# The stores of split rows move from SyncE's queue to GpSimd's, in an attention and two-network kernel

## The chip, the cores and the metric

The kernel runs on one core of a Trainium2 chip. The metric is the device time of the core in microseconds (us). Three runs of the kernel before took 730.86 to 731.88 us, with a median of 731.15. Short names of the engines: PE is TensorE, DVE is VectorE, ACT is ScalarE, POOL is GpSimd and SP is SyncE, which only issues DMAs here.

## The reference

Sparse attention feeds two dense networks, all in float32:

```
attn: 4 batches x 8 heads, 576 positions, head size 64, masked (local for 4 heads, strided for 4)
x   = attention output as 2304 tokens x 512
h   = max(x @ w1, x @ w2, x @ w3)        # first network, 512 -> 768
x2  = h @ w_out                          # 768 -> 512
h   = x2 @ w_in                          # second network, 512 -> 2048
g   = max(h, 0) + alpha * min(h, 0)
out = g @ w_out                          # 2048 -> 512
```

## The kernel before, in words

Each float32 factor of a matmul is held as a pair of a high part (a rounded copy) and a low part (what the rounding left), each [128, n]. A product is three matmuls per block: high x high, high x low, low x high (`PAIRS`). A split of rows is therefore two steps: a cast to the high part, and a subtraction for the low part.

The first network works batch by batch. Attention and the first three batches are ordered by a planner (`Weave`), which is over at about 300 us. The last batch is written out by hand in `last_net`: twelve gate units, 42 products (`product`, L913), and eight output products (L762) whose results are the tokens x2. They go to DRAM.

A product of `last_net` is 6 matmuls, an output product 18. Their results come in PSUM banks, eight of which are used in turn. The 42 products are six groups of seven. The first result of a group is copied by ACT (L931); the others are added and compared by DVE (L893). The last group ends in rows of h, split by ACT (L926, high) and DVE (L900, low). Every output product reads all rows of h, those of the last group last.

The second network works on three blocks of 768 tokens, numbered 0, 1 and 2, by a scheme of seven products for a 2 x 2 block matrix (`PRODUCTS`). Its x side needs seven row combinations for each of two halves, so fourteen split tiles of [128, 2, 384] per block. For block 0 they are made just before use. For blocks 1 and 2 they are made early, stored to DRAM (`xd`) and fetched again (`fetch_x2`, L1026) shortly before the block begins. A split tile is 384 KB.

Block 1's fourteen are made in the loop around `last_net`, in two halves. `early_load` (L982, SP) loads four pieces of x2 rows into two tiles `xs`, `early_sums` (L991) makes four sums on POOL, in part in the tiles `xs` themselves, and `early_split` casts a high part on ACT (L233) and subtracts the low part on POOL (L236), for seven parts numbered 0 to 6. The split tiles `xst` come from two pools of two buffers, used in turn: the cast of part k waits until the store of part k - 4 has landed. One unit of `last_net` after each split, `early_store` (L1020) issues its store. The second half's `early_load` goes into the same two tiles `xs`, so it waits for the low parts of the first half. The same pool `xsp`, and `xst`, later hold the x2 rows for block 0 (`load_x2`, L982).

Block 2's fourteen are made inside the second network, a step at a time: high part on ACT (L1443), some steps later the low part on DVE (L1435), and at its end `early_store`.

Each engine runs its own instructions in program order, and so does SP's queue of DMA issues: an issue that waits holds those behind it. SP issues every DMA of this kernel: weights (L852 for the last batch, L1034 and L1046 for the second network), rows, stores of x2 (L773) and of the result (L1193).

Of the kernel before, what the change touches and what calls it, by code (L numbers as in the profile page):

```python
# [10 lines left out]
F32 = mybir.dt.float32  # L11
# [161 lines left out]
def attention_maxout_prelu_kernel(  # L173
# [13 lines left out]
    nc = tc.nc  # L187
# [54 lines left out]
    def pool(stack, name, bufs, side="left"):  # L242
# [6 lines left out]
    xd = [None] + [[[dram.tile([P, 2, HB], F32, name=f"xd{blk}_{k}_{i}") for i in range(2)]  # L249
                    for k in range(7)] for blk in range(1, NBLK)]  # L250
# [766 lines left out]

    def early_store():
        for blk, k, i, t in early_parts:
            nc.sync.dma_start(xd[blk][k][i], t.bitcast(F32))  # L1020
        early_parts.clear()

    def fetch_x2(blk, k):
# [93 lines left out]
    for n, _ in enumerate(last_net(B - 1)):  # L1117
        if n in fetched:
            load_ow()
        if n - 1 in ready:  # L1120
            early_store()
        for half in range(2):
            if n == X_SPLIT + 21 * half - 8:
                early_load(1, half, xsp, "xs")
            if n == X_SPLIT + 22 * half - 2:
                early_sums(1, half)
        if n in ready:
            early_split(*ready[n], (xst, xsu)[n // 2 % 2])
        if n == gates - 5:
            rows = [load_x2(0, 0, xsp, "xs"), load_x2(0, 1, xst, "xst")]  # L1130
        if n == gates - 1:
            sx.close()
            x0x.close()
            xmp = pool(ctx, "xmp", 1, "right")
        if n == gates:
            sum_x2(0, 0, rows[0], nc.vector)
        if n == gates + 1:
            sum_x2(0, 1, rows[1], nc.vector)
        for i, ks in {0: [(0, range(7))], 2: [(1, range(4))], 3: [(1, range(4, 7))]}.get(n - gates, []):
            for k in ks:  # L1140
                x2h[0, k, i] = split_x2(0, k, i, xmp, f"x{k}{i}")
# [291 lines left out]
    def low_part(half, k):  # L1433
        t, x = high_parts.pop((half, k))
        nc.vector.tensor_tensor(out=t[:, 1], in0=x, in1=t[:, 0].bitcast(F32), op=ALU.subtract)  # L1435
        early_parts.append((2, k, half, t))
        if (half, k) != (0, 6):
            early_store()
# [12 lines left out]
    for half in range(2):  # L1451
        for n, i in steps[half][:4]:
            at(n, i, lambda: sums_left.pop(0)())
        for k, (n, i) in enumerate(steps[half][4:]):
            at(n - (i == 1), 4 if i == 1 else 2, lambda half=half, k=k: high_part(half, k))
            at(n, i, lambda half=half, k=k: low_part(half, k))
    at(NQ - 1, 0, early_store)

    outs = iter(())
    for n in range(NQ * NBLK):  # L1460
        blk, q = divmod(n, NQ)
# [72 lines left out]
```

## Time and profile before

| | |
|---|---|
| median of three runs | 731.15 us |
| profiled execution | 731.31 us, of which 729.5 us span |
| PE busy | 716.4 us (98%) |
| DVE busy | 615.0 us (84%) |
| ACT busy | 446.0 us (61%) |
| POOL busy | 30.3 us (4%), 53 instructions |
| DMA | 214.46 MB, mean 294 GB/s; nearly all on one queue, SP's |
| stores of split rows | 28 issues from SP of 384 KB |

The span goes from the first instruction to the last; the rest of an execution's time lies around it. Busy shares are means over the whole span. What an engine waits for is told in the waits and, in the timeline, in brackets behind an instruction: how long its engine stood idle before it, and what released it.

### The profile page before, as it was taken

The numbers are of one execution on the slowest core, as the hardware profiler recorded it, in microseconds if no ns is written. First come the engines' busy times: TensorE is split into PE (matmuls) and PEld (weight loads), VectorE is DVE, ScalarE is ACT, GpSimd is POOL, SyncE is SP. The second block draws the span as 40 slices with busy tenths as digits, with TensorE's granted clock in tenths as the row PEclk, the third lists the DMA queues.
The fourth block names the chain that finished last, engine by engine and source line by source line (L and its number), as shares of the span: only waits on it lengthen the run. The fifth ranks groups of instructions, "written<-read, shape, count | busy, mean of one in ns | idle before, by whom it ended". The sixth has DMA issues, their size and how long they took to land.

```text
span 729.5 us, 18174 instructions
## 1 busy us (share of the span) xinstructions
PE 716.4 (98%) x6682; PEld 698.0 (96%) x6682; DVE 615.0 (84%) x1680; ACT 446.0 (61%) x1180; POOL 30.3 (4%) x53
## 2 busy tenths in 40 slices
PE   8999999999999999899999999999999999999998
PEld 5899999999999999899989999999999999999997
DVE  6998987988989997588678988979988888888896
ACT  7988975876784784243356675626566644656561
POOL 2000000000000000065000000000000000000000
PEclk9999999999999999999999999999999999999999
DMA  8777599879999688698999799999789999867362
GB/s 296 271 274 232 176 310 344 312 277 308 327 358 343 229 278 290 224 319 321 367 331 339 250 332 328 404 392 357 252 301 318 370 400 354 302 228 264 108 201 68
DMA packets 90089, 214.46 MB, mean 294 GB/s; under 512 B 11152, under 2 KB 41360, under 8 KB 90000
## 3 DMA queue, kind: packets, MB, share of 16 engines
q1 hardware_dynamic: 90000, 213.30, 82.8%
q8 instruction: 53, 0.87, 0.5%
q14 instruction: 36, 0.29, 0.1%
HBM read 157.16 MB, written 56.10 MB: 292 GB/s over the span
## 4 chain that ended last, share of the span: by engine, by line
PE 92%; DVE 3%; ACT 3%; DMA 2%; issue 1%; SPq 0%; DVEq 0%; ACTq 0%
PE ph L1369 24%; PE bank L740 24%; PE po L1170 15%; PE bank L762 10%; PE bank L913 4%; PE po L1176 4%; PE ph L1170 4%; PE po L1180 2%; PE bank L426 1%; DMA wp<-w 1%; PE bank L352 1%; PE bank L465 1%; ACT es L487 1%; PE bank L535 1%; DMA raw<-in_w 1%
## 5 line engine op out<-in xcount | busy, mean ns | idle before, releaser
L740 PE MATMUL bank<-x,w 128*128 128x288 f32 x1440 | 199.4, 298 | 3.4 <-DVE t L751 3.2
L1369 PE MATMUL ph<-x,w 128*128 128x384 f32 x990 | 199.6, 336 | 0.8 <-ACT xo L969 0.8
L740 PEld LDWEIGHTS bank<-x,w 128*128 128x128 f32 x1440 | 193.5, 190 | 5.2 <-DVE t L751 3.5
L1369 PEld LDWEIGHTS ph<-x,w 128*128 128x128 f32 x990 | 166.6, 188 | 1.8 <-ACT xo L969 1.0
L1170 PE MATMUL po<-w,g 128*128 128x256 f32 x936 | 135.9, 282 | 0.0
L1170 PEld LDWEIGHTS po<-w,g 128*128 128x128 f32 x936 | 130.1, 190 | 0.3
L1375 DVE TENSOR_TENSOR c<-ph,c 128x384 f32<-128x384 f32 x165 | 89.3, 554 | 30.6 <-PE ph L1369 27.0
L1163 ACT CAST g<-c 128x384 fp32r<-128x384 f32 x93 | 47.0, 505 | 90.8 <-DVE c L1353 51.6
L762 PE MATMUL bank<-h,w 128*128 128x288 f32 x576 | 80.0, 297 | 0.0
L762 PEld LDWEIGHTS bank<-h,w 128*128 128x128 f32 x576 | 77.0, 189 | 0.4
L286 DVE TENSOR_TENSOR w<-word,w 128x512 fp32r<-128x512 f32 x100 | 63.6, 643 | 13.2 <-ACT w L283 12.5
L283 ACT CAST w<-word 128x512 fp32r<-128x512 f32 x100 | 57.6, 587 | 24.7 <-DMA wp<-w 8.5
L1313 ACT ACTIVATE c<-c 128x384 f32<-128x384 f32 x96 | 50.6, 527 | 32.9 <-DVE c L1375 31.8
L1314 ACT ACTIVATE c<-c,nalpha 128x384 f32<-128x384 f32 x96 | 59.3, 618 | 3.1
L1318 DVE SCALAR_TENSOR_TENSOR c<-c 128x384 f32<-128x384 f32 x96 | 53.0, 552 | 5.9 <-ACT c L1314 5.9
L1164 DVE TENSOR_TENSOR g<-c,g 128x384 fp32r<-128x384 f32 x96 | 52.9, 551 | 0.9 <-ACT g L1163 0.5
L1164 DVE TENSOR_TENSOR g<-k,g 128x384 fp32r<-128x384 f32 x72 | 37.0, 552 | 7.4 <-ACT g L1163 7.4
L1176 PE MATMUL po<-w,g 128*128 128x512 f32 x120 | 42.8, 396 | 0.0
L590 ACT ACTIVATE word<-raw 128x512 f32<-128x512 f32 x56 | 36.8, 675 | 5.7 <-DMA raw<-in_w 4.6
L830 DVE TENSOR_TENSOR t<-bank,t 128x288 f32<-128x288 f32 x72 | 32.6, 453 | 7.8 <-PE bank L740 3.8
L1353 DVE TENSOR_TENSOR k<-c 128x384 f32<-128x384 f32 x72 | 37.9, 550 | 0.0
L1163 ACT CAST g<-k 128x384 fp32r<-128x384 f32 x72 | 33.1, 514 | 7.1 <-PE po L1176 3.3
(123 smaller groups left out, 898.4 us busy)
## 6 DMA issues: line engine op xcount, KB each, us to landing
w<-wh SPq DMA_DIRECT2D x72, 512.0 KB, 5.4
raw<-in_w SPq DMA_DIRECT2D x50, 512.0 KB, 5.0
w<-wo SPq DMA_DIRECT2D x48, 512.0 KB, 5.9
w<-wp SPq DMA_DIRECT2D x36, 512.0 KB, 5.8
wh<-w SPq DMA_DIRECT2D x24, 512.0 KB, 4.8
xd<-xst SPq DMA_DIRECT2D x28, 384.0 KB, 3.0
x<-xd SPq DMA_DIRECT2D x28, 384.0 KB, 8.3
ws<-w SPq DMA_DIRECT2D x12, 512.0 KB, 4.6
```

Of the source, the lines that this page charges most:

```text
L283: (nc.scalar.copy if e == "ACT" else nc.vector.tensor_copy)(out_, in_)
L286: nc.vector.tensor_tensor(out=out_, in0=x, in1=y, op=ALU.subtract)
L740: nc.tensor.matmul(acc, words["gate", f, g][:, wi, cc * P:(cc + 1) * P], xt[b, cc, hf][:, xi, :], start=n == 0, stop=n == 3 * NCC - 1)
L762: nc.tensor.matmul(acc, words["mix", f][:, wi, dc * P:(dc + 1) * P], st["h", hf, f][:, xi, :], start=n == 0, stop=n == 3 * NF1 - 1)
L1163: cast(g[:, 0], x)
L1164: return g, lambda: nc.vector.tensor_tensor(out=g[:, 1], in0=x, in1=g[:, 0].bitcast(F32), op=ALU.subtract)
L1170: nc.tensor.matmul(bank[:, NH * half:NH * (half + 1)], g[:, gi, t * P:(t + 1) * P], w[:, wi, off:off + NH], start=first and i == 0, stop=l ...
L1176: nc.tensor.matmul(bank.rearrange("p (s n) -> p s n", n=NH), g[:, 0, t * P:(t + 1) * P], w[:, :, off:off + NH], start=first, stop=last)
L1314: nc.scalar.activation(a, a, AF.Copy, scale=nalpha[:, f:f + 1])
L1318: nc.vector.scalar_tensor_tensor(out=a, in0=h, scalar=0.0, in1=a, op0=ALU.max, op1=ALU.add)
L1369: nc.tensor.matmul(bank, words["h", n, i][:, wi, off + c * P:off + (c + 1) * P], x2h[blk, k, c][:, xi, :], start=m == 0, stop=m == 5)
L1375: nc.vector.tensor_tensor(out=out_, in0=bank, in1=other, op=ALU.add)
```

## The change

The function `early_store` issues its DMAs from POOL's queue and no longer from SP's. Its calls stay where they were, so on POOL the store of a part of block 1 stands between that part's low part and the next one's. Both uses are changed: block 1's stores and block 2's.

```diff
     def early_store():
         for blk, k, i, t in early_parts:
-            nc.sync.dma_start(xd[blk][k][i], t.bitcast(F32))
+            nc.gpsimd.dma_start(xd[blk][k][i], t.bitcast(F32))
         early_parts.clear()
```

## Rows read from the trace of the kernel before

**Rows 1.** The page, part 1: busy us (share of the span) and instructions of each engine.

```profile
PE 716.4 (98%) x6682; PEld 698.0 (96%) x6682; DVE 615.0 (84%) x1680; ACT 446.0 (61%) x1180; POOL 30.3 (4%) x53
```

**Rows 2.** Chain of waits in order of time: start us, length us, what.

```profile
319.40 30.42 PE bank L913 x227
349.82 17.13 PE bank L762 x129
```

**Rows 3.** Timeline of PE, 300 to 376 us: start, length, instruction, [idle before <-releaser].

```profile
318.87 30.95 PE L913 MATMUL bank<-x,w 128*128 128x288 f32 x228 [0.40 <-ACT x L233]
349.65 19.26 PE L762 MATMUL bank<-h,w 128*128 128x288 f32 x144
369.67 2.37 PE L1369 MATMUL ph<-x,w 128*128 128x384 f32 x12 [0.76 <-ACT xo L969]
372.59 2.36 PE L1369 MATMUL po<-x,w 128*128 128x384 f32 x12 [0.55 <-ACT xo L969]
```

**Rows 4.** Stretches: length, PE, PEld, DVE, ACT, POOL busy (x), clock, DMA, GB/s.

```profile
308.60:320.00 11.40, 10.78 (x65) 10.34 (x66) 9.06 (x20) 5.88 (x17) 5.54 (x6) 0.85 0.92 331
400.00:420.00 20.00, 20.00 (x136) 20.00 (x135) 18.55 (x39) 12.45 (x25) 0.00 (x0) 1.00 0.74 256
```

**Rows 5.** Line 1020: ns min/median/max, first and last start; waiter; landing.

```profile
L1020 SPq DMA_DIRECT2D xd<-xst x28: 319/320/548, 318.4 to 567.2; - x28
...
  ACT xst L233: 7.0, 6
...
DMA to landing us min/median/max: 2.3/3.0/7.6
```

**Rows 6.** Waits of SP's queue: us in total, times, longest.

```profile
SPq L1020 <- DVE xst L1435: 24.7, 13, 2.5
...
SPq L1020 <- POOL xst L236: 19.3, 11, 7.5
```

**Rows 7.** Timeline of POOL, 306 to 372 us; L991 sums, L236 low parts.

```profile
319.94 1.03 POOL L236 TENSOR_TENSOR xst<-t,xst 128x384 fp32r<-128x384 f32 x1 [1.54 <-ACT xst L233]
...
324.97 1.23 POOL L236 TENSOR_TENSOR xst<-xs,xst 128x384 fp32r<-128x384 f32 x1
335.71 1.02 POOL L991 TENSOR_TENSOR t<-xs 128x384 f32<-128x384 f32 x1 [9.50 <-DMA xs<-x]
...
340.12 1.02 POOL L236 TENSOR_TENSOR xst<-xs,xst 128x384 fp32r<-128x384 f32 x1
...
342.07 1.24 POOL L236 TENSOR_TENSOR xst<-xs,xst 128x384 fp32r<-128x384 f32 x1
...
346.98 1.01 POOL L236 TENSOR_TENSOR xst<-xs,xst 128x384 fp32r<-128x384 f32 x1 [0.31 <-ACT xst L233]
```

**Rows 8.** Timeline of ACT, 306 to 372 us.

```profile
328.33 0.40 ACT L931 COPY t<-bank 128x288 f32<-128x288 f32 x1 [3.43 <-PE bank L913]
...
346.39 0.51 ACT L233 CAST xst<-xs 128x384 fp32r<-128x384 f32 x1 [1.30 <-DMA xd<-xst]
...
356.67 0.51 ACT L233 CAST x<-xs 128x384 fp32r<-128x384 f32 x1 [3.02 <-DMA xs<-x]
```

**Rows 9.** Timeline of SP's issues, 306 to 372 us.

```profile
326.60 2.78 SPq L982 DMA_DIRECT2D xs<-x  x4
...
353.18 3.32 SPq L982 DMA_DIRECT2D xst<-x  x4
```

**Rows 10.** Line 982, the four loads issued at 306.1 to 308.7 us: landing.

```profile
DMA to landing us min/median/max: 2.3/2.4/2.5
```

**Rows 11.** Line 982, the last two loads, issued from 328.2 us: durations; landing.

```profile
L982 SPq DMA_DIRECT2D xs<-x x2: 452/572/693, 328.2 to 328.9; - x2
...
DMA to landing us min/median/max: 6.7/6.8/6.8
```

**Rows 12.** Timeline of DVE, 346 to 352.5 us.

```profile
347.23 1.02 DVE L893 TENSOR_TENSOR t<-bank,t 128x288 f32<-128x288 f32 x2 [0.24 <-ACT t L931]
...
351.21 0.45 DVE L900 TENSOR_TENSOR h<-t,h 128x288 fp32r<-128x288 f32 x1
```

## The prediction

> **What bounds the kernel now.** I read the page's busy shares first: TensorE (PE) is busy 716.4 of 729.5 us, POOL 30.3 us in 53 instructions [rows 1]. The chain of waits comes next: between 319.40 and 366.95 us it is two unbroken pieces of PE [rows 2]. Then PE's own timeline over 300 to 376 us: from 314 us on it stands 0.40, 0.76 and 0.55 us, each time for ScalarE (ACT) and never for a DMA [rows 3]. The stretches behind it show PE full, as in 400 to 420 us: 20.00 of 20.00 [rows 4]. So the stores can give back at most 0.40 + 0.76 + 0.55 = 1.71 us, and anything they delay far enough is paid in full.
>
> **The change part by part.** 28 issues of L1020 leave SP's queue and go to POOL's [rows 5]. On SP they took 0.32 us each, 9 us in all, and 24.7 + 19.3 us of waiting for the low parts [rows 5, 6], with other loads queued behind. PE waited for none of those loads [rows 3, 4], so this removal is worth nothing on the path; the loads' cover is their own buffers, issued several products ahead.
>
> *Fourteen stores of block 2* (414.5 to 567.2 us). POOL has nothing else there, 0.00 us in 400 to 420 us [rows 4]. High part on ACT, low part on DVE and the store are steps apart. ACT waited for a store six times, 7.0 us in all, and all six belong to block 1's cast (L233), the last at 346.39 [rows 5, 8]. Cost 0, hidden by an idle POOL and the distance between steps; without that cover each store would be late by D (below), and still not PE.
>
> *Fourteen stores of block 1* (from 318.4 us [rows 5] to 348). This is where POOL has work: it makes the four sums and the seven low parts of each half [rows 7], and each store now stands on POOL between one low part and the next. The unknown is D, how long a store holds POOL. From below, SP's 0.32 us; from above, POOL held until the data have landed, 3.0 us median [rows 5]. The nearest row is POOL's own instruction on this tile, 1.01 to 1.03 us and stretched to 1.24 [rows 7]. I take D = 1.1, a little over the unstretched ones for the hand-over, because the store becomes one more instruction of POOL, which serves this tile shape in that time.
>
> The Trainium skill gives a price that no row has: in "DMA: Bandwidth & Descriptors", section "Latency and other measured facts", a first byte comes after about 1 us from GpSimd's queue and about 0.6 us from SyncE's. With 1.0 for D the sum below would be 0.8 us shorter, an estimate from that page.
>
> First half. Low part 1 starts at 319.94 either way (store 0 fits into the 1.54 us of idle before it) and ends at 320.97. Then five stores and five low parts: 320.97 + 5 x (1.1 + 1.03) = 331.6, against 326.2 before (324.97 + 1.23) [rows 7]. ACT's casts for parts 4 to 6 wait for stores 0 to 2 and come some 2 us later; the next thing on ACT, the copy at 328.33, had waited 3.43 us for PE [rows 8], so this is absorbed. But the tiles that the low parts read are those that the next half's rows are loaded into (L982). Before, SP issued those at 326.60 to 329.4, they needed 6.7 us, and POOL's sums began at 335.71 [rows 7, 9, 11]. Now the second pair can't go before 331.6 and (0.45 us an issue, the shortest of these) 332.05. It finds a nearly empty queue, since SP has stood at that very wait, with only the first pair ahead of it; for the same load the rows have 2.4 us near 306 us and 6.7 us near 329 us [rows 10, 11]. I take 3.0, near the empty queue's row, as only the stores run beside it: the sums begin at 335.1, 0.6 us earlier than before, because the old queue was fuller.
>
> Second half. Sums 4.41 us (335.71 to 340.12 [rows 7]) end at 339.5. Three low parts with their stretches, 3.19 us (340.12 to 343.31), and two stores between them, 2.2 us: low part 2 ends at 344.9, its store leaves POOL at 346.0. Landing after that: SP's stores took 2.3 us at best and 3.0 median from issue [rows 5], 2.0 to 2.7 without the 0.32 us of issue; I take 2.4. So ACT's cast of part 6 starts at 348.4 in place of 346.39: 2.0 us late. As a formula, 339.57 + 8 x D against 346.39.
>
> What is queued behind it: ACT's copy (L931), for which DVE's add at 347.23 waited [rows 12]. DVE then runs without a gap worth the name to the low part of h that ends at 351.66 [rows 12]. The first output product starts at 349.65 and spends 0.134 us per matmul (19.26 over 144 [rows 3]); its 17th, at 351.79, reads that low part. Slack 0.1 us, so PE stands for 1.9 us. PSUM doesn't stop it before: with eight banks, the bank that the late copy frees is wanted by the second output product, at 352.1.
>
> After that: low part 6 ends at 354.0 (339.5 + 7.87 us for seven low parts, 340.12 to 347.99, + 6 x 1.1 us), store 6 lands at 357.5. Block 0's rows wait for those tiles: their last loads were issued by 356.5 [rows 9] and now go at about 358.3, 1.8 us later. That hides behind PE's own 1.9 us; without that stall it would be the next thing late, as PE waits for ACT at 369.67 already [rows 3].
>
> A rule could shorten this. Before, a store could take long behind loads in the same queue: 2.3 us at best, up to 7.6 [rows 5]. The Trainium skill ("DMA: Bandwidth & Descriptors", "Queues, rings and completion order") says that each DMA engine takes turns between queue rows, packet by packet, so a store in its own row would not stand behind SP's loads. By that rule landing would be at its 2.0 us, and the sum 0.4 us less. No run here shows it yet.
>
> Sum: +1.9 us on the path of the profiled execution, 729.5 of span plus 1.8 around it, 731.31 us. It lies 0.16 us over the median of 731.15, so 731.15 + 1.9 = 733.1 us.
>
> **The rivals.** (a) *POOL is held too briefly to matter.* With D near SP's 0.32 us the second half starts at 335.7 as before and the cast comes at 340.12 + 3.19 + 3 x 0.32 + 2.4 = 346.67, 0.3 us late: +0.2 us, 731.3. For it: SP's row. Against it: nothing on POOL that touches this tile takes under 1.0 us. (b) *POOL is held longer than one such instruction.* At D = 1.9 the formula gives 354.8, +8.3 us after the slack, 739.4; with rows landing in 6.7 in place of 3.0 us it is +5.6 at my own D. A stall of this size may also cost clock: between 308.6 and 320 us, where PE has just begun again after pauses, the granted clock is 0.85 over 11.4 us [rows 4], some 1.7 us. For it: eight D stand on the path, so each tenth of a microsecond is 0.8 us. (c) *Faster, by SP's freed queue.* Without 44 us of waiting on SP the rows for block 0 could land earlier, ACT's splits at 356.67 (3.02 us waiting for such rows [rows 8]) move up, and PE's pauses at 369.67 and 372.59 shrink. It decides if POOL's low parts end no later than before; the price is 1.3 us, 1.7 with the pause at 318.87, so 729.5 to 729.9. Against it: those loads are held by the low parts, which the stores push back. (d) *The change does nothing*, because SP's stores were hidden and POOL's are too, whatever D: that is (a)'s time, and the ACT waits of 7.0 us speak against it.
>
> **How the numbers follow.** Forecast 0.52 (+0.6 to +5 us, D of 0.95 to 1.45), (a) with (d) 0.26, (b) 0.14, (c) 0.08. A measurement of this kernel tells 0.2% (1.46 us) from no change. Of the forecast's chance 0.40 lies above that and 0.12 below. Slower: 0.40 + 0.14 = 0.54. Faster by over 1.46 us needs nearly all of the 1.71 us: 0.06 of (c). Same: 0.12 + 0.26 + 0.02 = 0.40. The range goes from 730.6 (within it all of (a)) to 737.5 (D near 1.7), leaving out (c)'s far end and most of (b). The forecast's own range is 731.7 to 736.
>
> **What would show it.** In the new profile: no L1020 on SP; starts of POOL's low parts 2.1 us apart in place of 1.0; the last one of the first half ending near 331.6 and the sums starting near 335.1; ACT's waits for the stores growing by some 2 us per half; a new PE wait of about 1.9 us in the first output product, on DVE's low part of h at L900; and PE otherwise as before up to the end. Low parts 1.3 us apart would be (a); over 2.8, (b). The prediction is wrong in its path if the casts come 2 us late and PE doesn't stop near 351.7, and wrong in its size if the spacing is right but the rows for the second half land at another time than 335.

## The result, and the profile after

The changed kernel took 740.4 us (median of 4 runs, 738.44 to 741.56), the kernel before, run beside it, 731.51 us (4 runs, 730.86 to 732.11). The ratio is 1.0119 with a 95% interval of 1.0095 to 1.0143: slower by 8.9 us, outside the predicted range. The profiled run took 738.44 us, 7.1 us more than before, with a span of 736.4 us.

The busy time of POOL grows as the change says, to 81 instructions [rows 1], and the 28 stores have a queue of their own, q0 (page, parts 1 and 3: queue, packets, MB, share of the 16 DMA engines):

```profile
PE 719.3 (98%) x6682; PEld 700.2 (95%) x6682; DVE 620.0 (84%) x1680; ACT 446.5 (61%) x1180; POOL 45.8 (6%) x81
...
q0 software_dynamic: 2240, 11.01, 3.7%
```

**Where PE lost it.** PE's timeline after, from 314 us, against [rows 3]:

```profile
314.82 3.34 PE L913 MATMUL bank<-x,w 128*128 128x288 f32 x24
318.74 30.96 PE L913 MATMUL bank<-x,w 128*128 128x288 f32 x228 [0.58 <-ACT x L233]
349.54 1.78 PE L762 MATMUL bank<-h,w 128*128 128x288 f32 x12
354.71 1.03 PE L762 MATMUL bank<-h,w 128*128 128x288 f32 x3 [3.40 <-ACT h L926]
356.53 20.40 PE L762 MATMUL bank<-h,w 128*128 128x288 f32 x129 [0.79 <-ACT h L926]
376.77 2.27 PE L1369 MATMUL ph<-x,w 128*128 128x384 f32 x12
```

Up to 349.54 us nothing is lost (349.65 before). Then PE stands in the first output product, where the prediction put it, for 3.40 + 0.79 us; and the 129 matmuls behind the stall take 20.40 us where before, at 19.26 us for 144, as many took 17.25. The runs below are compared by the stretch that holds all of this, from the first matmul of L913 to the first of L1369: 54.53 us before (315.14 to 369.67), 61.95 after. Of its growth of 7.42 us, 3.61 is idle time of PE (4.77 against 1.16) and 3.81 lies in the matmuls: 3.15 in the 129 behind the stall (20.40 against 17.25), and 0.63 in the three between the two waits, which take 1.03 us where 3 x 0.134 = 0.40 would do. The granted clock says why most of them are slower: it is between TensorE's two levels, 1.2 GHz (0.50) and 2.4 GHz (1.00), over the stretches from 350 us (columns as in [rows 4]), first before:

```profile
350.00:358.00 8.00, 8.00 (x62) 8.00 (x61) 3.65 (x10) 2.11 (x5) 0.00 (x0) 1.00 1.04 369
358.00:366.00 8.00, 8.00 (x63) 8.00 (x62) 6.99 (x14) 3.59 (x9) 0.00 (x0) 1.00 0.99 332
```

and after:

```profile
350.00:358.00 8.00, 3.69 (x17) 2.69 (x16) 5.86 (x14) 2.62 (x6) 3.69 (x5) 0.88 0.89 300
358.00:366.00 8.00, 8.00 (x46) 8.00 (x45) 7.25 (x16) 4.84 (x12) 0.00 (x0) 0.70 0.75 230
```

In the second line PE is busy all 8.00 us in both kernels, but does 46 matmuls in place of 63.

**What PE waited for.** The timeline of POOL after, against [rows 7]: L1020 is the store.

```profile
323.62 1.02 POOL L236 TENSOR_TENSOR xst<-t,xst 128x384 fp32r<-128x384 f32 x1
324.94 0.56 POOL L1020 DMA_DIRECT2D xd<-xst  x1 [0.30 <-POOL xst L236]
325.52 1.02 POOL L236 TENSOR_TENSOR xst<-xs,xst 128x384 fp32r<-128x384 f32 x1
...
330.06 1.02 POOL L236 TENSOR_TENSOR xst<-xs,xst 128x384 fp32r<-128x384 f32 x1
...
336.25 1.00 POOL L991 TENSOR_TENSOR t<-xs 128x384 f32<-128x384 f32 x1 [4.30 <-DMA xs<-x]
...
342.81 1.03 POOL L236 TENSOR_TENSOR xst<-t,xst 128x384 fp32r<-128x384 f32 x1
344.24 0.56 POOL L1020 DMA_DIRECT2D xd<-xst  x1 [0.41 <-POOL xst L236]
344.82 1.03 POOL L236 TENSOR_TENSOR xst<-xs,xst 128x384 fp32r<-128x384 f32 x1
```

A store costs POOL 0.56 us and, ahead of it, 0.30 to 0.41 us of waiting for the low part that POOL has just made: low parts are 1.9 us apart in the first half, 2.0 in the second. Then the timeline of ACT after, against [rows 8]: the casts of parts 4, 5 and 6, each waiting for a store to land, and the copy behind them.

```profile
347.97 0.51 ACT L233 CAST xst<-xs 128x384 fp32r<-128x384 f32 x1 [6.66 <-DMA xd<-xst]
350.14 0.51 ACT L233 CAST xst<-t 128x384 fp32r<-128x384 f32 x1 [1.66 <-DMA xd<-xst]
351.17 0.51 ACT L233 CAST xst<-xs 128x384 fp32r<-128x384 f32 x1 [0.51 <-DMA xd<-xst]
351.58 0.39 ACT L931 COPY t<-bank 128x288 f32<-128x288 f32 x1
```

And the landing of the three stores that they wait for (line 1020 after, issued from 342.2 to 346.3 us; the same three took 2.3, 2.3 and 3.0 us before):

```profile
DMA to landing us min/median/max: 4.8/5.7/5.8
```

Measured from the first matmul of L913, the cast of part 6 came at +31.25 us before and at +36.35 after, 5.10 later. That is 0.86 from the sums (+20.57, now +21.43), 2.21 from the spacing of the low parts (part 2: +26.93, now +30.00, 3.07 later), and 2.03 from the landing (from the start of low part 2 to the cast, 4.32 and now 6.35 us).

The last link is DVE. One of its steps in the timeline before, and the same stretch after, against [rows 12]:

```profile
348.29 0.46 DVE L893 TENSOR_TENSOR t<-t 128x288 f32<-128x288 f32 x1
```

```profile
352.01 1.02 DVE L893 TENSOR_TENSOR t<-bank,t 128x288 f32<-128x288 f32 x2 [1.80 <-ACT t L931]
353.06 1.13 DVE L893 TENSOR_TENSOR t<-t 128x288 f32<-128x288 f32 x1
...
354.69 0.46 DVE L900 TENSOR_TENSOR h<-t,h 128x288 fp32r<-128x288 f32 x1
...
356.66 0.45 DVE L900 TENSOR_TENSOR h<-t,h 128x288 fp32r<-128x288 f32 x1
```

DVE made up none of the delay. Its add that waits for the copy started 4.78 us later in the profile's time, and the low part of h that ended at 351.66 before now ends at 357.11 (356.66 + 0.45), 5.45 later, as a step between them took 1.13 us in place of 0.46. PE reads four new pieces of h in the first output product, and in order: its waits of 3.40 and 0.79 us are for the two high parts, and the two low parts (354.69 and 356.66) come while it is at the matmuls behind each wait. The 17th matmul, which reads the last of them, starts at 357.17 us.

The landing is long because SP no longer waits (the experiments test this). SP's issues after:

```profile
326.57 5.35 SPq L982 DMA_DIRECT2D xs<-x  x4
332.01 0.98 SPq L852 DMA_DIRECT2D w<-ws  x2
333.08 11.39 SPq L1034 DMA_DIRECT2D w<-wh  x6
349.91 4.83 SPq L982 DMA_DIRECT2D xs<-x  x4
```

Six loads of wh go out by 344.47 us, and their landings take 5.5 to 8.4 us, so that two or three of them are in flight when each of the three stores is issued. Before, two of the six went at 332.73 us and the next at 344.06 and 348.58, because they stood behind stores that waited for low parts.

### The profile page after: what moved, and what is told of

Same layout as the page of the kernel before. It is cut to its first block, busy times and chain, and to the rows that moved or that the text cites. A ratio compares the mean times of both kernels' runs of the same rounds, so it can differ in the third digit from the quotient of the medians.

```text
span 736.4 us, 18183 instructions
## 1 busy us (share of the span) xinstructions
PE 719.3 (98%) x6682; PEld 700.2 (95%) x6682; DVE 620.0 (84%) x1680; ACT 446.5 (61%) x1180; POOL 45.8 (6%) x81
## 5 line engine op out<-in xcount | busy, mean ns | idle before, releaser
L1369 PE MATMUL ph<-x,w 128*128 128x384 f32 x990 | 199.4, 336 | 0.3 <-ACT c L1379 0.3
L1369 PEld LDWEIGHTS ph<-x,w 128*128 128x128 f32 x990 | 166.6, 188 | 1.3 <-ACT c L1379 0.5
L762 PE MATMUL bank<-h,w 128*128 128x288 f32 x576 | 83.8, 304 | 4.3 <-ACT h L926 4.2
L762 PEld LDWEIGHTS bank<-h,w 128*128 128x128 f32 x576 | 79.8, 194 | 5.7 <-ACT h L926 4.7
```

The costliest lines, as they stand in the source:

```text
L762: nc.tensor.matmul(acc, words["mix", f][:, wi, dc * P:(dc + 1) * P], st["h", hf, f][:, xi, :], start=n == 0, stop=n == 3 * NF1 - 1)
L1369: nc.tensor.matmul(bank, words["h", n, i][:, wi, off + c * P:off + (c + 1) * P], x2h[blk, k, c][:, xi, :], start=m == 0, stop=m == 5)
```

## The experiments

Each row gives the ratio to the kernel before in the same session with its interval; then, from one profile each, by how many us the stretch above grew over 54.53, how much of that is PE idle, and the rest, when idle time and unused matmuls are taken off; and by how much later the cast of part 6 came, measured from the first matmul of L913. Where that matmul starts differs from profile to profile, 314.5 to 319.0 us, also in kernels whose stretch is unchanged, so the stretch and not the span is compared. The rest is lost clock for the most part and not in all: e9_fill, whose clock stays at 1.00, has 0.6 us there, and a matmul alone between two waits takes 0.40 us in place of 0.134. One profile stands for each run and need not be typical: the profiled execution took 740.68 us in e3_first3, whose median is 736.58, and 741.58 in e6_gated, whose median is 738.73.

| run | ratio (95%) | stretch | idle | rest | cast 6 |
|---|---|---|---|---|---|
| the change | 1.0119 (1.0095 to 1.0143) | +7.42 | +3.61 | 3.8 | +5.10 |
| e1_block1 | 1.0076 (1.0051 to 1.0100) | +5.97 | +3.14 | 2.8 | +5.33 |
| e2_block2 | 1.000 (0.998 to 1.002) | +0.52 | +0.54 | 0.0 | |
| e3_first3 | 1.0059 (1.0038 to 1.0079) | +6.14 | +2.43 | 3.7 | +3.60 |
| e4_last4 | 1.0053 (1.0035 to 1.0072) | +5.00 | +1.32 | 3.7 | +1.79 |
| e5_held | 1.0092 (1.0063 to 1.0120) | +5.43 | +2.24 | 3.2 | +3.42 |
| e6_gated | 1.0088 (1.0064 to 1.0111) | +8.12 | +4.12 | 4.0 | +6.42 |
| e7_act | one run, 741.7 us | +8.47 | +5.66 | 2.8 | |
| e9_fill | 1.0060 (1.0038 to 1.0081) | +4.54 | +0.55 | 0.6 | +4.95 |
| e11_one_gate | 1.0089 (1.0066 to 1.0113) | +7.50 | +3.89 | 3.6 | +5.95 |
| e12_gate_fill | 1.0092 (1.0072 to 1.0113) | +6.09 | +1.53 | 2.8 | +4.58 |
| e13_late_gate | 1.0095 (1.0073 to 1.0118) | +5.54 | +2.21 | 3.3 | +2.66 |
| e14_late_fill | 1.0103 (1.0086 to 1.0119) | +6.25 | +2.03 | 2.5 | +2.84 |

**Which stores.** The two parts of the change alone, in the kernel before:

```diff
-            nc.sync.dma_start(xd[blk][k][i], t.bitcast(F32))
+            (nc.gpsimd if blk == 1 else nc.sync).dma_start(...)   # e1_block1
+            (nc.gpsimd if blk == 2 else nc.sync).dma_start(...)   # e2_block2
```

> Only block 1's fourteen stores go from POOL, block 2's from SP. Theory (the whole loss is made by block 1's stores, through ACT's cast waiting for them and PE's stall in the first output product, and the lower clock behind it): +7 to +9 us against before, the same as the change, with a PE wait of about 4 us for the split of h near 351 us. Rival (block 2's stores cost a share, ACT's cast at L1443 waits 6.6 us for them in the changed kernel): 2 us or more less than the change.

> Only block 2's fourteen stores go from POOL. Theory: within 1 us of before, PE without a new wait, though the stores land in about 4.9 us at the median (2.6 to 3.0 from SP). Rival: they cost 2 us or more.

Block 1's stores alone bring most of the loss, 5.6 us by the ratio, and block 2's alone none. That is less than the +7 to +9 us expected, and 3.3 us less than the change, as e1_block1's rival had it. The rival's cause isn't seen, though: e2_block2 loses nothing, and behind the stretch the change's profile takes no longer than that of before (359.6 and 359.9 us to the end). Where the 3.3 us lie stays open; the two intervals just overlap. Block 2's stores do take long to land (median 4.8 us on POOL's queue) and ACT waits 5.1 us for them in all (L1443), but PE doesn't; its timeline in e2_block2 runs through the output products:

```profile
352.82 19.23 PE L762 MATMUL bank<-h,w 128*128 128x288 f32 x144
373.33 2.38 PE L1369 MATMUL ph<-x,w 128*128 128x384 f32 x12 [1.28 <-ACT xo L969]
```

**Which of block 1's stores.** Only three per half on POOL, or only the other four; three are those that the casts of parts 4 to 6 wait for.

```diff
+            (nc.gpsimd if blk == 1 and k < 3 else nc.sync).dma_start(...)   # e3_first3
+            (nc.gpsimd if blk == 1 and k > 2 else nc.sync).dma_start(...)   # e4_last4
```

> Of block 1, only the stores of parts 0 to 2 of each half go from POOL, those for which the casts of parts 4 to 6 wait. Theory (the long landing of these three stores, 5 to 6 us in place of 2.3 to 3.0, is what reaches PE): most of the loss stays, +5 us or more, casts of part 6 in the second half near 350 us. Rival (POOL's time for all seven stores delays low parts and with them the rows): POOL holds three stores of seven, so the loss is under half, +3 us or less.

> Of block 1, only the stores of parts 3 to 6 of each half go from POOL; those of parts 0 to 2 stay on SP. Theory (landing of stores 0 to 2): loss gone, within 1.5 us of before, ACT's waits for the stores at about 7 us as before. Rival (POOL's time): four stores of seven, half of the loss or more, +4 us.

Neither is without loss. In e3_first3 POOL's three stores of the second half land in 2.6 us, since SP is again held by the other four; but so is the load of the next rows (issued from 331.92 us), and the sums start at +22.72 us. Its 4.3 us by the ratio lie between the two expectations. In e4_last4 the three stores land in 2.4 to 2.7 us from SP, and the cast is only 1.79 us late, all of which is there already when the sums start (+22.47 us, 1.90 later). PE waits less (1.40 + 0.63 us), yet the 129 matmuls behind the waits take nearly the 20.40 us of the change:

```profile
355.21 20.13 PE L762 MATMUL bank<-h,w 128*128 128x288 f32 x129 [0.63 <-ACT h L926]
```

That the loss would be gone here was a miss; the rival's +4 us came (3.9 by the ratio).

**POOL's time alone.** All stores stay on SP; POOL writes an unused tile three times behind each of block 1's low parts, 1.1 us for the three.

```diff
             nc.sync.dma_start(xd[blk][k][i], t.bitcast(F32))
+        if early_parts and early_parts[0][0] == 1:
+            for _ in range(3):
+                nc.gpsimd.memset(spare, 0.0)           # spare: [128, 280]
         early_parts.clear()
```

> All stores on SP as before; after each of block 1's low parts POOL runs three memsets of a spare tile in place of the store (about 0.9 us, what a store held POOL in the changed kernel). Theory A (POOL's time alone makes the loss): low parts 1.9 to 2.0 us apart, and +4 us or more. Theory B (POOL's time is a part, and the landing of the stores in the presence of SP's loads another): the stores land in 2.3 to 3 us, ACT's cast of part 6 in the second half comes 1 to 2 us later in the stretch than before, and the loss is +1 to +3 us.

The figures of theory A came: low parts 2.04 us apart, and +5.4 us in the stretch, 6.7 by the ratio. POOL and PE of e5_held:

```profile
325.69 1.11 POOL L1023 MEMSET spare<- 128x280 f32 x3
326.77 1.01 POOL L236 TENSOR_TENSOR xst<-t,xst 128x384 fp32r<-128x384 f32 x1
...
341.31 1.02 POOL L991 TENSOR_TENSOR t<-xs 128x384 f32<-128x384 f32 x1 [6.14 <-DMA xs<-x]
```

```profile
356.49 0.40 PE L762 MATMUL bank<-h,w 128*128 128x288 f32 x1 [2.30 <-ACT h L926]
357.20 0.53 PE L762 MATMUL bank<-h,w 128*128 128x288 f32 x2 [0.31 <-DVE h L900]
358.52 20.54 PE L762 MATMUL bank<-h,w 128*128 128x288 f32 x129 [0.79 <-ACT h L926]
```

The low parts are spaced nearly as in the change. The second half's stores 0 to 2 land fast (2.3 to 2.9 us), but the first half's stand in SP's queue ahead of the rows, whose load goes only at 334.51 us. So POOL's time is enough for a loss of this size, but isn't alone here: with the stores on SP the rows come late as well, where in the change the landings are long.

**The landing.** In e6_gated each store on POOL is followed by a 3 KB store of the same tile from SP, so that SP is held as before. In e7_act block 1's stores go from ACT's queue.

```diff
             nc.gpsimd.dma_start(xd[blk][k][i], t.bitcast(F32))
+            if blk == 1:                       # e6_gated, against the change
+                nc.sync.dma_start(gate[k][i], t[:1].bitcast(F32))
...
-            nc.sync.dma_start(xd[blk][k][i], t.bitcast(F32))
+            (nc.scalar if blk == 1 else nc.sync).dma_start(...)       # e7_act, against before
```

> As the change, but behind each of block 1's stores on POOL, SP issues a store of 3 KB (one partition of the same tile), so that SP's queue waits for the low part as before and holds the loads behind it. Theory B (the long landing is the collision with loads that the freed SP queue issues): stores of parts 0 to 2 land in about 2.6 us in place of 4.8 to 6, ACT's waits for them fall from 15.7 us towards 9, and 2 us or more of the loss go. Rival (a store from POOL's queue lands late by itself): landing stays near 5 us and the time near the change's.

> Block 1's stores from ACT's queue, block 2's from SP's: a second queue, as the change has, but not POOL's. One look at the landing only, since ACT itself now waits for POOL's low parts and the time must rise by some 5 us. Theory B (collision with the loads of a freed SP queue): landing of parts 0 to 2 of 4 us or more in at least some of the six, as from POOL. Rival (POOL's queue lands late by itself): 2.3 to 3.0 us for all six.

The landings of stores 0 to 2 of the second half fall to 2.6, 2.6 and 4.0 us in e6_gated, so SP's loads made them long. That 2 us or more of the loss would go was a miss: the ratio's interval overlaps the change's. SP, held, issues the rows at 332.76 us, the sums start at +23.94 and the cast is 6.42 us late. From ACT's queue the same stores took 3.5 to 5.1 us: the long landing isn't POOL's own.

Two more runs hold SP at one place only. In e11_one_gate the 3 KB store follows the second half's part 2; in e13_late_gate it follows part 4, and SP's loads for the last groups are issued one group later, so that they stand behind it.

```diff
             nc.gpsimd.dma_start(xd[blk][k][i], t.bitcast(F32))
+            if (blk, k, i) == (1, 2, 1):       # e11_one_gate
+            if (blk, k, i) == (1, 4, 1):       # e13_late_gate
+                nc.sync.dma_start(gate, t[:1].bitcast(F32))
...
-            load_factors(k + 4)                # in last_net, e13_late_gate only
+            late_loads.append(k + 4)
+            for kk in late_loads[:-1] if k > NP + 1 else late_loads[:]:
+                load_factors(kk)
+                late_loads.remove(kk)
...
+                for kk in late_loads:          # behind the last group
+                    load_factors(kk)
```

> The change, with one store of 3 KB from SP behind the second half's part 2, so that SP holds the second network's weight loads (L1034) until POOL has made that part, and nothing else. Theory (the landing of the second half's stores 0 to 2 in 4.8 to 5.8 us, made by those loads, is one of the terms): they land in 2.6 to 3.5 us, the cast of part 6 comes some 2 us earlier after the first product of L913 than the change's 36.4 us, and the stretch from there to the first product of the second network falls from 61.95 by 1.5 to 2.5 us. Rival (what is saved at the landing comes back as late rows or loads): landing short, stretch as long.

> The change with one small (3 KB) store from SyncE's queue behind the second half's low part 4, and SyncE's loads for the last groups deferred behind it, so that SyncE's queue is held until the second half's stores 0, 1 and 2 have gone out; the first half is as in the change, so the rows are not issued later than there. Theory 1 (the long landing, 4.8 to 5.8 us, comes from the loads that the freed SyncE queue sends out meanwhile, and adds about 2 us to the cast of part 6): stores 0 to 2 of the second half land in 2.5 to 3.0 us, the cast of part 6 starts 1.5 to 3 us earlier against the first product of L913 than in the change (33.5 to 35 us in place of 36.35), PE's idle time in the stretch from the first L913 matmul to the first L1369 matmul falls from 4.8 to 2 to 3.5 us, and the stretch from 61.95 to 58.5 to 60.5 us; ratio to the kernel before 1.004 to 1.007. Theory 2 (the landing only fills time that something else, such as the late rows or DVE's chain, would set anyway): landings fall, the stretch stays at 61 to 62.5 us, ratio 1.008 to 1.012.

e11_one_gate missed: the first two stores land in 2.6 us, then the held loads go out at 346.64 us, together with the third, which takes 5.4; the cast comes later than in the change. In e13_late_gate all three are alone; SP's issues and the three landings:

```profile
327.73 4.60 SPq L989 DMA_DIRECT2D xs<-x  x4
332.43 0.94 SPq L853 DMA_DIRECT2D w<-ws  x2
333.46 1.61 SPq L1043 DMA_DIRECT2D w<-wh  x2
350.94 0.30 SPq L1029 DMA_DIRECT2D gate<-xst  x1
```

```profile
DMA to landing us min/median/max: 2.6/2.6/2.6
```

The cast comes 2.44 us earlier than in the change, and PE:

```profile
350.68 1.78 PE L763 MATMUL bank<-h,w 128*128 128x288 f32 x12
353.75 0.40 PE L763 MATMUL bank<-h,w 128*128 128x288 f32 x1 [1.30 <-ACT h L928]
355.28 0.85 PE L763 MATMUL bank<-h,w 128*128 128x288 f32 x2 [1.12 <-DVE h L901]
356.60 19.72 PE L763 MATMUL bank<-h,w 128*128 128x288 f32 x129 [0.48 <-ACT h L928]
```

By landing, cast, idle time and stretch theory 1 holds: without the long landing PE is idle 2.21 us more than before, 1.4 less than in the change. The ratio, 1.0095, is above the 1.004 to 1.007 expected and in the range of theory 2 (1.008 to 1.012), and its interval overlaps that of the change: a gain in time from the short landing is not shown. In this profile 1.6 us of the loss lie outside the stretch, 0.95 ahead of it and 0.6 behind.

**The clock.** Unused matmuls of 224 columns, whose results nothing reads, fill PE's wait in the first output product: 28 in the changed kernel (e9_fill), 14 on top of e11_one_gate (e12_gate_fill) and of e13_late_gate (e14_late_fill).

```diff
-    def out1_products(b, hf, dc, st):
-        acc = bank()[:, :HALF]
+    def out1_products(b, hf, dc, st, fill=0):   # 28 or 14 for hf == dc == 0
+        full = bank()
+        acc = full[:, :HALF]
         n = 0
+        for _ in range(fill):
+            nc.tensor.matmul(full[:, HALF:], words["mix", 0][:, 0, :P],
+                             st["h", hf, 0][:, 0, :512 - HALF], start=True, stop=True)
```

> As the change, with 28 matmuls of 224 columns whose results are not used (about 2.9 us) ahead of the first output product, so that PE works where it stood 3.4 us in the changed kernel. Theory (of the loss in the stretch some 3.9 us are the lower clock behind the stall): the granted clock stays at 1.00 from 350 to 366 us and 2 to 4 us of the change's loss go. Rival (the stall itself is the loss, the clock follows anyway): the time as the change's, within 1 us.

> The change with that one store from SP and 14 matmuls without use (1.5 us) ahead of the first output product. Theory: landing and clock are both taken away and what is left is POOL's time for the stores: stretch of 56.5 to 58.5 us (54.53 before, 61.95 with the change), clock 1.00 over 350 to 366 us, +2 to +4 us against before. Rival (the loss is one and the same whatever the landing and the clock): over 60 us.

> As the last one, with 14 unused matmuls of 224 columns (1.6 us at 3.2 us for 28) ahead of the first output product; their results are read by nothing. If the rest of the loss is PE's short stall and the clock that falls behind it: granted clock 0.95 to 1.00 in 350 to 366 us, PE's idle time in the stretch 1.2 to 2.2 us, stretch 56.5 to 58.5 us and ratio 1.001 to 1.004. If the clock does not depend on the length of the stall: clock 0.85 or below in 350 to 366 us and stretch 59.5 to 61 us, as without them.

PE and the granted clock in e9_fill:

```profile
349.96 3.39 PE L762 MATMUL bank<-h,w 128*128 128x224 f32 x28 [0.28 <-DVE t L897]
353.18 2.15 PE L766 MATMUL bank<-h,w 128*128 128x288 f32 x15
355.90 0.40 PE L766 MATMUL bank<-h,w 128*128 128x288 f32 x1 [0.56 <-ACT h L930]
356.53 17.22 PE L766 MATMUL bank<-h,w 128*128 128x288 f32 x128 [0.23 <-DVE h L904]
```

```profile
350.00:358.00 8.00, 7.20 (x55) 6.75 (x56) 7.64 (x15) 2.36 (x6) 3.34 (x5) 1.00 0.89 295
358.00:366.00 8.00, 8.00 (x62) 8.00 (x62) 7.23 (x16) 4.48 (x12) 0.00 (x0) 1.00 0.77 246
```

The stores, the landings and the late cast (4.95 us) are the change's, yet with the wait filled the clock stays at 1.00 and the stretch shrinks by 2.88 us; the ratio falls from 1.0119 to 1.0060. So the fall of the clock follows from PE standing, and it costs about 2.9 us of the stretch; the other 4.54 us stay, as the chain from POOL is as late as it was. Half the fill was not enough: e14_late_fill left waits of 1.12 + 0.79 + 0.24 us behind it, and the clock still fell:

```profile
358.00:366.00 8.00, 8.00 (x51) 8.00 (x51) 4.16 (x9) 2.60 (x7) 0.00 (x0) 0.81 0.81 288
```

Its stretch, 60.78 us, and that of e12_gate_fill, 60.62 (waits of 2.21 + 0.48 left; its third store still took 5.2 us to land), missed what was expected of them: in both the figures of the other reading came (59.5 to 61 us with a clock of 0.85 or below; over 60 us). Neither ratio is below that of the same kernel without the fill.

A last run filled an earlier place, in the kernel before, ahead of a gate unit, with 24 unused matmuls:

> The kernel before, all stores on SP, with 24 matmuls of 224 columns whose results are not used (2.5 us) ahead of the gate unit at which PE stands 3.2 us before 308.7 us. Theory (a stall costs its length and then 2 to 4 us of lower clock, which work without use in its place saves): the granted clock over 310 to 320 us rises from 0.85 to 1.00 and the time falls by 1 to 2 us. Rival (the clock falls there for what lies before the stall): no change, or slower by what the matmuls take.

The fill itself had to wait 11.13 us for its bank, the clock fell to 0.61 in 310 to 320 us, and the ratio was 1.013 (1.0109 to 1.0151). It tells nothing on that pause.

## Why the prediction was wrong

Its mechanism was right: which stores matter, the path from POOL through ACT's cast and copy and DVE to the first output product, block 2 at nothing, SP's relief worth nothing, and PE undisturbed up to 350 us. Its slack of 0.1 us holds too: the low part of h (L900) that it named is the last piece that PE waits for, and ends 5.45 us later than before; the 17th matmul starts right behind it. As the chain is so late, PE stands for the earlier pieces as well, and the idle time is put down to those, ACT's high parts (L926). Block 0's rows, late but hidden, were right: PE's 0.76 us at L1369 is gone.

D was right in size, 1.1 us where 0.9 to 1.0 was measured, but in part by luck: it was taken from a tensor instruction on this tile, and what holds POOL is 0.56 us of issue and 0.30 to 0.41 us of waiting ahead of it. The rival that set its 739.4 by D = 1.9 had the time nearly right and the cause wrong.

Three terms of the sum failed:

1. *The landing.* The sum took 2.4 us after POOL is free. The three stores took 4.8 to 5.8 us from issue, and the path from low part 2 to the cast grew by 2.03 us where the prediction had 0.4. The prediction had read that loads stood on SP behind waiting stores, and took that as worth nothing since no one waits for those loads. That they would then run over the stores was not asked. The Trainium skill's rule of turns between queue rows ("DMA: Bandwidth & Descriptors", "Queues, rings and completion order") was read as no delay; this case's traces show 2.6 us with SP held and 4.8 to 5.8 us with two or three of its loads in flight, from a row of its own. That fits taking turns, and not the reading.
2. *The start of the sums*, put 0.6 us earlier, came 0.86 later: the rows' four loads landed in 3.1 to 4.6 us, and not in 3.0, with stores and loads beside them.
3. *The clock*, left out of the sum and named in a rival at 1.7 us, cost about 3 us: 2.9 by e9_fill; the 129 matmuls behind the stall, which also hold the wait for the last low part, grew by 3.15. This is the largest. In e13_late_gate landings are as short as the prediction had them, the cast is 2.66 us late (predicted: 2.0) and PE's idle time grows by 2.21 us (predicted: 1.9); the stretch still grows by 5.54 us, with 2.5 of the rest in the 129 matmuls (19.72 us against 17.25).

So of the 7.42 us some 2.9 are clock, which the sum put at nothing, and 4.54 are the late chain (e9_fill), which it put at 1.9. The chain is longer than predicted by the landing (1.6 us on the way to the cast) and the sums (1.5). What the long landing alone costs in device time no run shows: without it PE is idle 1.4 us less (3.61 less 2.21) in one profile, and the ratio is not clearly lower. Between the medians lie 8.9 us; the 1.8 us beyond the profiled runs' difference are not explained.

## What to carry to other kernels

An issue that waits in an in-order queue is also a gate: before taking it out, list the transfers it holds back and ask whom they will meet once they run free. A DMA on a compute engine's queue can cost that engine its issue and the wait for its own last result, on POOL here 0.9 to 1.0 us each, and eight in a row on one chain decide. And where a new wait will stop a full PE for some 2 us, price the clock behind it from the start: here it cost about 3 us, with waits of 4.19 us in the change and of 2.03 in e4_last4.

## What the runs showed of the hardware that was not expected

- What the lower clock costs doesn't follow the length of the waits. The 129 matmuls behind them, with any short wait for the last low part, took 17.25 us before, 20.13 behind waits of 1.40 + 0.63 us (e4_last4), 19.72 behind 1.30 + 1.12 + 0.48 (e13_late_gate) and 20.40 behind 3.40 + 0.79 (the change). Behind 1.12 + 0.79 + 0.24 us (e14_late_fill) and behind 2.04 + 0.79 + 0.23 (e1_block1) the last 128 took 18.76 both times, where 17.12 is the time before. With waits of 0.56 + 0.23 us in the place nothing fell: 17.22 for 128 (e9_fill).
- A store of 384 KB landed 2.6 us after POOL's issue with SP's queue held, and 4.8 to 5.8 us with two or three weight loads of SP in flight; from ACT's queue 3.5 to 5.1 us.
- POOL waits 0.30 to 0.42 us between the end of its own low part and the store that reads it.
